# One PSUM tile per bank in the second layer, two-bank operations cut in two, buffers assigned by a table

## The chip, the cores and the metric

The kernel runs on one core of a Trainium2 chip. The metric is the device time of one execution in microseconds; the median of three runs is shown, and one more execution was taken with the hardware profiler. TensorE is called PE here (PEld is its weight load), VectorE is DVE, ScalarE is ACT, GpSimd is POOL and SyncE is SP.

## The reference

Three stages in a row, all in fp32, on 4 batches of 576 tokens (2304 tokens), model width 512, inner width 1536:

```python
x = _attn_ref(q, k, v, phi)              # attention over 32 memory slots
x = x.transpose(0, 2, 1, 3).reshape(2304, 512)
x = (x @ w_a) * (x @ w_b) @ w_out        # first layer
g = x @ w_gate                           # second layer
return (g * (1 / (1 + np.exp(-g)))) * (x @ w_val) @ w_out2
```

## The kernel before

**Stages.** Attention and the first layer fill the first 405 us. The second layer (from 405 us to the end) is written as units. A unit `U b.i` is one batch `b` (0 to 3) and one slice `i` (12 to 23) of 128 inner columns. It forms the gate and value columns for 576 tokens from seven products of half-size blocks instead of eight; each product (`product(n)`) is six matmuls of 128x288, since every fp32 operand is split in a high and a low part. Units of batches 0 and 1 run side by side for all `i`, then those of batches 2 and 3, so there are 24 pairs of units and 48 units. `H j.i.t` is a tile of the last matmul: 6 matmuls of 128x512, 108 such tiles in all, spread between the units; its result is added into an SBUF sum (line 829).

**PSUM in the second layer.** Each of the two units that run side by side (`o` is 0 or 1) has one PSUM tile of three banks, `chain0` or `chain1`; the banks are called A, C and Z. A third tile of two banks serves the `H` tiles, which use its banks in turn:

```python
for o in range(2):
    chain.append(ps2.tile([128, 3, 512], FP32, tag=f"chain{o}", name=f"chain{o}"))
chain.append(ps2.tile([128, 2, 512], FP32, tag="p4", name="p4"))
```

**The steps of a unit before,** in the order of the code, with the engine, the bank and the line. Product 5 into Z; ACT copies Z (769). Product 1 into A; ACT copies A to `gate` (774). Product 2 into C; DVE adds the copy onto C (778). Product 6 is accumulated onto A; ACT copies A (782). Product 3 is accumulated onto Z; DVE adds that copy onto Z (786). ACT takes the sigmoid of C and Z in one instruction of 576 elements (789), DVE multiplies by it, 576 elements (791). Product 7 is accumulated onto A; DVE writes A plus the copy of Z into C (795). Product 4 is accumulated onto A; DVE multiplies A and C by the result of 791, 576 elements (799). ACT casts the result to its high part (805), DVE forms the low part (807). Lines 761 and 507 are the matmuls of the products and of the `H` tiles.

**Order and waits.** The order of all instructions is written out as a list of words, `PLAN`, that a search made; each word runs one step of a generator, and each engine takes its instructions in the order of the list. Waits between engines are put in by the tile framework: it follows which instruction reads and writes which tile. Buffers come from pools that hand out the next free one. Weights of the second layer are decoded during the first pass (lines 209 to 262), stored to DRAM, and read again for each pass (lines 144 to 167). Words `z` are matmuls of the identity whose result nobody reads (`warm`, line 700); there are 15 in the list, most of them near its start.

Of the kernel before, what the change touches and what calls it, by code (L numbers as in the profile page):

```python
# [18 lines left out]
def kernel(  # L19
# [21 lines left out]
    nc = tc.nc  # L41
# [20 lines left out]

    ident = const.tile([128, 128], FP32, name="ident")
# [35 lines left out]
    def bank2(name):  # L99
        return ps.tile([128, 2, 512], FP32, tag="b2", name=name)  # L100
# [30 lines left out]
    def w_hi(i, grp, x):  # L131

        k = GRP[grp][1]
        shape = [128, k, 2, 256]
        if grp in ("g", "u"):
            t = w_p.tile(shape, FP32R, tag="w", name=f"w_{grp}")
        elif "w2" not in late:
            n = 0 if grp == "t" else 1024
            t = half("h10 1", FP32R).rearrange("p a b -> p (a b)")
            t = t[:, n:n + k * 512].rearrange("p (k l f) -> p k l f", l=2, f=256)  # L140
        else:
            t = late["w2"].tile(shape, FP32R, tag=grp, name=f"w_{grp}")
        wb[i, grp] = t
        nc.scalar.copy(out=t[:, :, 0], in_=x)  # L144
# [5 lines left out]
    def o_hi(i, x):  # L150
        t = w_p.tile([128, 2, DM], FP32R, tag="o", name="o")
# [7 lines left out]
    def again(i):  # L159

        s = raw_p.tile([128, 4, 256], FP32, tag="raw", name="again_s")
# [3 lines left out]
        else:  # L165
            a = raw_p.tile([128, 3, 256], FP32, tag="raw", name="again_a")
# [9 lines left out]
    def again_out(i):  # L176
        o = raw_p.tile([128, DM], FP32, tag="raw", name="again_o")
# [7 lines left out]
    def chunk_load(c):  # L185
# [3 lines left out]
        t = raw_p.tile([128, 512, 2], I32, tag="raw", name="raw")  # L189
# [125 lines left out]
    def att_phi(b):  # L315
# [3 lines left out]
        m = at_p.tile([128, PR, M], FP32, tag="pm", name="pm")  # L319
# [5 lines left out]
        nmx = sm_p.tile([128, 2, 1], FP32, tag="nmx", name="nmx")  # L325
# [39 lines left out]
        rs = sm_p.tile([128, 2], FP32, tag="rs", name="rs")  # L365
# [3 lines left out]
        kv = at_p.tile([128, 3, 2, D], FP32, tag="kvm", name="kvm")  # L369
# [48 lines left out]
    def att_scores(b, t):  # L418
# [31 lines left out]
        mx = sm_p.tile([128, 2, R, 1], FP32, tag="mx", name="mx")  # L450
# [8 lines left out]
        den = sm_p.tile([128, 2, R, 1], FP32, tag="den", name="den")  # L459
# [60 lines left out]
    def vw_part(parts):  # L520
# [19 lines left out]
        for part, pv in zip(parts, pvs):  # L540
            f, b = part[0]
            if f > 1 or b not in vw_2:
                vw_2[b] = [
                    vw_p.tile([128, 2, 2, 256], FP32R, tag=f"vw{x}", name=f"vw{x}") for x in "hl"
                ]
            t = vw_2[b]
            o = int(f == 1)
            for n, (f, b) in enumerate(part):
                vw_t[b, f] = [x[:, o + n] for x in t]
            n = len(part)  # L550
            hi, lo = [x[:, o:o + n].rearrange("c n g x -> c g n x") for x in t]
            nc.scalar.copy(out=hi, in_=pv[:, :, 0:n])
            yield
            nc.vector.tensor_tensor(out=lo, in0=pv[:, :, 0:n], in1=f32(hi), op=ALU.subtract)
# [21 lines left out]
    def s1_b(b, f):  # L576
        pb = s1_product(b, f, 128, "s1b")
        yield
        bs = bs_p.tile([128, 2, HB], FP32, tag="t", name="bs")
# [6 lines left out]
        if n not in g_t:  # L586
            g_t[n] = [g_p.tile([128, 2 * S], FP32R, tag=f"g{x}", name=f"g{x}") for x in "hl"]
        g = [of_batch(x, half) for x in g_t[n]]
        nc.scalar.copy(out=g[0], in_=bs)
        yield  # L590
        eng("gl", B * f + b).tensor_tensor(out=g[1], in0=bs, in1=f32(g[0]), op=ALU.subtract)
# [137 lines left out]
    def second():  # L729
# [7 lines left out]
        for o in range(2):  # L737
            chain.append(ps2.tile([128, 3, 512], FP32, tag=f"chain{o}", name=f"chain{o}"))
        chain.append(ps2.tile([128, 2, 512], FP32, tag="p4", name="p4"))
        yield  # L740

    def unit(b, i):
        o, j = b % 2, b // 2

        def bank(n, m=1):
            p = chain[o][:, n:n + m, 0:HB]
            return p if m > 1 else p[:, 0]
# [17 lines left out]

        product(5)
        yield
        q5 = late["tmp"].tile([128, HB], FP32, tag="q", name="p5")
# [4 lines left out]
        g = late["tmp"].tile([128, 2, HB], FP32, tag="g", name="gate")  # L773
# [22 lines left out]
        yield  # L796
        product(4)
        yield
        tt(out=g, in0=bank(A, 2), in1=s, op=mul)  # L799
        yield  # L800
        if (j, i) not in g2_t:
            g2_t[j, i] = late["g2"].tile([128, 2, 2 * S], FP32R, tag="g2", name="g2")
# [7 lines left out]
    def s4_tile(j, i, t):  # L810
        cs = slice(t * 128, (t + 1) * 128)
        p = chain[2][:, t % 2]
# [26 lines left out]
    def x_of(b):  # L839
# [3 lines left out]
        if not temps:  # L843
            temps.append(late["g2"].tile([128, 2, UNIT], FP32, tag="g2", name="temp"))
# [238 lines left out]
```

## Time and profile before

| | |
|---|---|
| median of 3 runs | 982.66 us (977.31 to 985.5) |
| profiled execution: its own time | 991.04 us |
| its span, first to last instruction | 989.3 us |
| granted TensorE clock, mean over the span | 0.969 of full speed |
| PE busy, PEld busy | 863.1 us (87%), 772.3 us (78%) |
| DVE, ACT, POOL busy | 570.7, 401.8, 378.1 us |

A profiled execution is a single one, so its parts are summed against its own 991.04 us. Matmuls are pipelined: the busy time of PE counts the tail of each matmul beside the next one's start.

### The profile page before, as it was taken

What the parts mean: (1) busy time and instruction counts of PE and PEld (TensorE: products, weight loads), DVE (VectorE), ACT (ScalarE), POOL (GpSimd) and SP (SyncE); (2) the same over time, 40 slices, a digit from 0 to 9 for tenths busy, and PEclk for the clock granted to TensorE, in tenths of its full rate; (3) what the DMA queues carried; (4) which work ended last, traced back from release to release, by engine and by line L of the source; (5) the groups of instructions that cost most, each with busy time, mean ns of one, the idle gap of its engine ahead of it and who ended that gap; (6) DMA issues with size and microseconds to landing.
All of it is one profiled execution on the core that took longest, in us unless ns stands there. A gap on an engine that the chain in (4) does not pass through costs nothing.

```text
span 989.3 us, 16445 instructions
## 1 busy us (share of the span) xinstructions
PE 863.1 (87%) x6570; PEld 772.3 (78%) x6570; DVE 570.7 (58%) x924; ACT 401.8 (41%) x742; POOL 378.1 (38%) x319
## 2 busy tenths in 40 slices
PE   5899999999999999877879797888878887897876
PEld 4688999999999999766668676777768776786764
DVE  5789858777866667653345555446543244444353
ACT  3666555444544445445343433335334423232220
POOL 0445554445434355544244343433431322232100
PEclk9799999999999999998799999999999999999999
DMA  9963333443322124125233433320242120111103
GB/s 331 345 209 102 130 99 122 138 145 99 131 92 86 64 78 127 64 91 169 82 105 92 127 128 101 103 91 1 70 129 70 59 85 1 49 59 38 38 1 95
DMA packets 61772, 102.51 MB, mean 104 GB/s; under 512 B 6400, under 2 KB 35072, under 8 KB 61696
## 3 DMA queue, kind: packets, MB, share of 16 engines
q1 hardware_dynamic: 60896, 100.29, 31.4%
q8 instruction: 51, 0.84, 0.3%
q10 hardware_dynamic: 800, 1.18, 0.3%
q14 instruction: 25, 0.20, 0.1%
HBM read 82.58 MB, written 18.87 MB: 103 GB/s over the span
## 4 chain that ended last, share of the span: by engine, by line
PE 75%; DVE 12%; ACT 5%; issue 3%; DMA 2%; SPq 1%; POOL 1%; DVEq 0%; ACTq 0%; POOLq 0%
PE chain L761 25%; PE p L507 15%; PE s L507 12%; PE s1a L515 7%; PE s1b L515 7%; DVE h_2x L829 3%; PE vw L530 2%; PE s L515 2%; DVE g L807 2%; DVE gate L799 1%; DVE sig L791 1%; DMA raw<-in_moe_w_b_dram 1%; ACT gate L774 1%; PE sc L429 1%; ACT gate L782 1%
## 5 line engine op out<-in xcount | busy, mean ns | idle before, releaser
L507 PE MATMUL p<-o,g 128*128 128x512 f32 x648 | 175.6, 412 | 11.9 <-DVE h_2x L829 10.4
L507 PEld LDWEIGHTS p<-o,g 128*128 128x128 f32 x648 | 122.9, 199 | 40.7 <-DVE h_2x L829 16.1
L507 PE MATMUL s<-gh,o 128*128 128x384 f32 x480 | 126.4, 335 | 0.0
L829 DVE TENSOR_TENSOR h_2x<-p,h_2x 128x512 f32<-128x512 f32 (+1 forms) x100 | 61.4, 633 | 65.1 <-PE p L507 65.0
L235 POOL TENSOR_TENSOR dec_a<-dec_a,raw 128x512 int32<-128x512 int32 x48 | 64.1, 1339 | 89.9 <-DVE dec_a L223 60.7
L507 PEld LDWEIGHTS s<-gh,o 128*128 128x128 f32 x480 | 87.1, 188 | 0.4 <-DVE dec_a L219 0.4
L209 ACT ACTIVATE dec_a<-raw 128x512 f32<-128x512 f32 x72 | 48.0, 674 | 83.8 <-POOL w L233 22.6
L507 PE MATMUL s<-gl,o 128*128 128x384 f32 x240 | 80.3, 334 | 0.0
L515 PE MATMUL s1b<-h_1x,vwh 128*128 128x288 f32 x384 | 67.6, 298 | 0.3 <-DVE h_1x L488 0.3
L515 PE MATMUL s1a<-h_1x,vwh 128*128 128x288 f32 x384 | 67.3, 297 | 0.0
L786 DVE TENSOR_TENSOR chain<-chain,gate 128x288 f32<-128x288 f32 x48 | 22.3, 465 | 74.9 <-PE chain L761 72.4
L761 PE MATMUL chain<-h_x0x,w_g 128*128 128x288 f32 x288 | 48.7, 310 | 17.1 <-ACT gate L774 13.7
L148 POOL TENSOR_TENSOR w_g<-again_a,w_g 128x512 fp32r<-128x512 f32 x24 | 31.0, 1293 | 81.9 <-ACT w_g L144 81.9
L761 PE MATMUL chain<-h_x0x,w_u 128*128 128x288 f32 x288 | 49.1, 315 | 14.9 <-DVE sig L791 9.3
L799 DVE TENSOR_TENSOR gate<-chain,sig 128x576 f32<-128x576 f32 x48 | 35.9, 755 | 43.7 <-PE chain L761 39.8
L761 PEld LDWEIGHTS chain<-h_x0x,w_g 128*128 128x128 f32 x288 | 42.4, 196 | 23.1 <-ACT gate L774 17.4
L148 POOL TENSOR_TENSOR w_u<-again_s,w_u 128x512 fp32r<-128x512 f32 x24 | 31.1, 1296 | 76.2 <-ACT w_u L144 76.2
L761 PE MATMUL chain<-h_x1x,w_t 128*128 128x288 f32 x288 | 48.7, 307 | 13.1 <-DVE chain L778 8.7
L761 PE MATMUL chain<-h_x1x,w_g 128*128 128x288 f32 x288 | 48.3, 306 | 13.5 <-ACT gate L774 11.1
L761 PE MATMUL chain<-h_x1x,w_u 128*128 128x288 f32 x288 | 46.8, 305 | 15.1 <-DVE sig L791 13.1
L515 PEld LDWEIGHTS s1b<-h_1x,vwh 128*128 128x128 f32 x384 | 56.8, 188 | 2.7 <-issue 0.8
L761 PEld LDWEIGHTS chain<-h_x0x,w_u 128*128 128x128 f32 x288 | 43.3, 201 | 19.8 <-DVE sig L791 11.7
(209 smaller groups left out, 1929.2 us busy)
## 6 DMA issues: line engine op xcount, KB each, us to landing
raw<-in_moe_w_out_dram SPq DMA_DIRECT2D x24, 512.0 KB, 3.9
again_s<-dr_w SPq DMA_DIRECT2D x24, 512.0 KB, 4.4
dr_w<-dec_a SPq DMA_DIRECT2D x36, 256.0 KB, 2.6
again_a<-dr_w SPq DMA_DIRECT2D x24, 384.0 KB, 3.1
raw<-in_moe_w_a_dram SPq DMA_DIRECT2D x12, 512.0 KB, 3.8
raw<-in_moe_w_b_dram SPq DMA_DIRECT2D x12, 512.0 KB, 4.7
raw<-in_moe_w_val_dram SPq DMA_DIRECT2D x12, 512.0 KB, 3.9
raw<-in_moe_w_gate_dram SPq DMA_DIRECT2D x12, 512.0 KB, 3.9
```

The costliest lines, as they stand in the source:

```text
L148: nc.gpsimd.tensor_tensor(out=t[:, :, 1], in0=x, in1=f32(t[:, :, 0]), op=ALU.subtract)
L209: nc.scalar.activation(out=f32(a), in_=f32(hi), func=ACTF.Abs)
L235: nc.gpsimd.tensor_tensor(out=a, in0=a, in1=lo, op=ALU.add)
L429: nc.tensor.matmul(pc[cols, o, r * M:(r + 2) * M], lhsT=qT_t[b][:, j * (R // 2) + r // 2, cols], rhs=kb[b % 2][:, g, j].rearrange("c o m - ...
L507: nc.tensor.matmul(dst, lhsT=l, rhs=r, start=(i == 0), stop=(i == n - 1))
L515: nc.tensor.matmul(p[:, hb, 0:HB], l, x, start=(i == 0), stop=(i == n - 1))
L530: nc.tensor.matmul(pv[M * j:M * j + M, g, n], lhsT=vt[b][rows, M * j:M * j + M], rhs=whl[f][0][rows, j].rearrange("p t c -> p (t c)"), sta ...
L761: nc.tensor.matmul(bank(where), lhsT=x, rhs=y, start=first and t == 0, stop=t == len(terms) - 1, skip_group_check=True,)
L786: tt(out=bank(Z), in0=bank(Z), in1=g[:, 1], op=add)
L799: tt(out=g, in0=bank(A, 2), in1=s, op=mul)
L807: tt(out=lo, in0=v, in1=f32(hi), op=ALU.subtract)
L829: tt(out=dst, in0=src, in1=dst, op=add)
```

## The change

- Each bank of the second layer's PSUM is a tile of its own: `p_a0`, `p_c0`, `p_z0` for one unit, `p_a1`, `p_c1`, `p_z1` for the other, `p_h0` and `p_h1` for the `H` tiles.
- An instruction then can't span banks A and C or C and Z. The sigmoid, the multiplication by it and the last multiplication become two instructions of 288 elements each. The half on C now follows right behind the addition onto C, ahead of product 6; the half on Z follows behind the addition onto Z.
- Buffers of most pools are taken by a table (`SLOTS`): the n-th tile of a kind gets the buffer that the table names. Their numbers stay as they were.
- In the first layer the low halves of two kinds of tiles (`vwl`, `gl`) are taken when they are first written, not together with the high halves.
- The list of the order is another one throughout. The words `z` are gone from it.

```diff
+    SLOTS = """
...
+    bs 012101201201021201211020201102110120021102101202 gh
...
+    def ring(pool, shape, dt, tag, name, key=None):
+
+        key = key or tag
+        n = made[key] = made.get(key, -1) + 1
+        if key in slots:
+            return pool.tile(shape, dt, tag=f"{tag}_{slots[key][n]}", bufs=1, name=name)
+        return pool.tile(shape, dt, tag=tag, name=name)
...
-        for o in range(2):
-            chain.append(ps2.tile([128, 3, 512], FP32, tag=f"chain{o}", name=f"chain{o}"))
-        chain.append(ps2.tile([128, 2, 512], FP32, tag="p4", name="p4"))
+        for n in ("a0", "c0", "z0", "a1", "c1", "z1", "h0", "h1"):
+            chain.append(ps2.tile([128, 512], FP32, tag=n, name=f"p_{n}"))
         yield
...
-        def bank(n, m=1):
-            p = chain[o][:, n:n + m, 0:HB]
-            return p if m > 1 else p[:, 0]
+        def bank(n):
+            return chain[3 * o + n][:, 0:HB]
...
         tt(out=bank(C), in0=bank(C), in1=g[:, 0], op=add)
         yield
+        s = ring(t_p, [128, 2, HB], FP32, "s", "sig")
+        nc.scalar.activation(out=s[:, 0], in_=bank(C), func=ACTF.Sigmoid)
+        yield
         product(6)
         yield
         nc.scalar.copy(out=g[:, 1], in_=bank(A))
         yield
+        tt(out=s[:, 0], in0=bank(C), in1=s[:, 0], op=mul)
+        yield
         product(3)
         yield
         tt(out=bank(Z), in0=bank(Z), in1=g[:, 1], op=add)
         yield
-        s = late["tmp"].tile([128, 2, HB], FP32, tag="s", name="sig")
-        nc.scalar.activation(out=s, in_=bank(C, 2), func=ACTF.Sigmoid)
-        yield
-        tt(out=s, in0=bank(C, 2), in1=s, op=mul)
+        nc.scalar.activation(out=s[:, 1], in_=bank(Z), func=ACTF.Sigmoid)
         yield
         product(7)
         yield
         tt(out=bank(C), in0=bank(A), in1=q5, op=add)
         yield
+        tt(out=s[:, 1], in0=bank(Z), in1=s[:, 1], op=mul)
+        yield
         product(4)
         yield
-        tt(out=g, in0=bank(A, 2), in1=s, op=mul)
+        tt(out=g[:, 1], in0=bank(C), in1=s[:, 1], op=mul)
+        yield
+        tt(out=g[:, 0], in0=bank(A), in1=s[:, 0], op=mul)
         yield
...
     def s4_tile(j, i, t):
         cs = slice(t * 128, (t + 1) * 128)
-        p = chain[2][:, t % 2]
+        p = chain[6 + t % 2]
...
     PLAN = """
-    z11 P0 p0 p0 p0 P1 W0.0 p1 p0 K0 z9 z7 p1 c0.0 L0 Q0 c0.0 W0.1 z8 p0 p1 p0 z10 c0.1 c0.0 e0
+    P0 K0 W0.1 p0 p0 c0.1 p0 p0 L0 c0.1 W0.0 p0 p0 e0 p0 Q0 P1 c0.1 p0 c0.1 c0.0 W1.1 p0 W1.2 q0.0
...
```

**PE in the second layer, the units of slice 13.** Rows are matmuls: the bank's tile, the token and weight tiles, the shape, how many in a row, and in brackets the engines whose semaphore the row waits for. Weights `w_g` belong to products 1 and 2, `w_t` to 6 and 3, `w_u` to 5 and 7. Before, from product 2 of the second unit to product 7 of the first:

```order
L761 MATMUL chain1_4867<-h2_x0x_4751,w_g_4948 128x288 [waits Activation_49]
L761 MATMUL chain1_4867<-h2_x0x_4751,w_g_4948 128x288 x5
L761 MATMUL chain0_4866<-h3_x0x_4643,w_t_5001 128x288 x6
L761 MATMUL chain1_4867<-h6_x0x_4800,w_t_5001 128x288 [waits DVE_49]
L761 MATMUL chain1_4867<-h6_x0x_4800,w_t_5001 128x288 x5
L761 MATMUL chain1_4867<-h4_x0x_4695,w_t_5001 128x288 [waits Activation_49]
L761 MATMUL chain1_4867<-h4_x0x_4695,w_t_5001 128x288 x5
L761 MATMUL chain0_4866<-h3_x0x_4643,w_u_4907 128x288 [waits DVE_49]
L761 MATMUL chain0_4866<-h3_x0x_4643,w_u_4907 128x288 x5
L761 MATMUL chain0_4866<-h1_x0x_4636,w_u_5084 128x288 x2
L761 MATMUL chain0_4866<-h1_x0x_4636,w_u_5084 128x288 [waits Pool_49]
```

Now, from product 2 of both units to product 6 and 3 of both:

```order
L789 MATMUL p_c0_4839<-h0_x0x_4565,w_g_4919 128x288 x6
L789 MATMUL p_c1_4842<-h2_x0x_4723,w_g_4919 128x288 x6
L789 MATMUL p_a0_4838<-h1_x0x_4583,w_t_4967 128x288 [waits Activation_49]
L789 MATMUL p_a0_4838<-h1_x0x_4583,w_t_4967 128x288
L789 MATMUL p_a0_4838<-h1_x0x_4583,w_t_4967 128x288 [waits Pool_49]
L789 MATMUL p_a0_4838<-h1_x0x_4583,w_t_4967 128x288 x3
L789 MATMUL p_a1_4841<-h6_x0x_4770,w_t_4967 128x288 [waits Activation_49]
L789 MATMUL p_a1_4841<-h6_x0x_4770,w_t_4967 128x288 x5
L789 MATMUL p_z1_4843<-h4_x0x_4644,w_t_4967 128x288 x6
L789 MATMUL p_z0_4840<-h3_x0x_4634,w_t_4967 128x288 x6
L789 MATMUL p_a0_4838<-h3_x0x_4634,w_u_4908 128x288 [waits Activation_49]
L789 MATMUL p_a0_4838<-h3_x0x_4634,w_u_4908 128x288 x5
```

Product 2 (`w_g`, into C) has lost its wait for ACT and stands for both units ahead of product 6; product 3 (`w_t`, into Z) has lost its wait for ACT; product 6 (`w_t`, onto A) waits for ACT, which copied A, and no longer for DVE.

**DVE at the same place.** Rows are the additions and multiplications of both units: 778, 786, 795, 791 and 799 before. Before:

```order
L786 TENSOR_TENSOR chain0_4866<-chain0_4866,gate_5049 128x288 [waits PE_49,Activation_49]
L778 TENSOR_TENSOR chain1_4867<-chain1_4867,gate_5076 128x288 [waits Activation_49]
L791 TENSOR_TENSOR sig_5100<-chain0_4866,sig_5100 128x576 [waits Activation_49]
L786 TENSOR_TENSOR chain1_4867<-chain1_4867,gate_5076 128x288 [waits PE_49,Activation_49]
L795 TENSOR_TENSOR chain0_4866<-chain0_4866,p5_5027 128x288 [waits DVE_49,PE_49]
L791 TENSOR_TENSOR sig_5134<-chain1_4867,sig_5134 128x576 [waits Activation_49]
L799 TENSOR_TENSOR gate_5049<-chain0_4866,sig_5100 128x576 [waits DVE_49,PE_49]
L795 TENSOR_TENSOR chain1_4867<-chain1_4867,p5_5031 128x288 [waits DVE_49,PE_49]
L219 TENSOR_SCALAR dec_a_5029<-dec_a_5029 128x512
L223 SCALAR_TENSOR_TENSOR dec_a_5029<-raw_4692,dec_a_5029 128x512 [waits DVE_49]
L799 TENSOR_TENSOR gate_5076<-chain1_4867,sig_5134 128x576 [waits PE_49]
```

Now lines 807, 820 and 826 are the additions, 816 and 828 the multiplications by the sigmoid, 832 and 834 the last multiplications:

```order
L807 TENSOR_TENSOR p_c0_4839<-p_c0_4839,gate_5043 128x288 [waits PE_49,Activation_49]
L807 TENSOR_TENSOR p_c1_4842<-p_c1_4842,gate_5048 128x288 [waits PE_49,Activation_49]
L816 TENSOR_TENSOR sig_5080<-p_c1_4842,sig_5080 128x288 [waits Activation_49]
L816 TENSOR_TENSOR sig_5069<-p_c0_4839,sig_5069 128x288
L820 TENSOR_TENSOR p_z1_4843<-p_z1_4843,gate_5048 128x288 [waits PE_49,Activation_49]
L820 TENSOR_TENSOR p_z0_4840<-p_z0_4840,gate_5043 128x288 [waits PE_49,Activation_49]
L826 TENSOR_TENSOR p_c0_4839<-p_a0_4838,p5_5015 128x288 [waits DVE_49,PE_49]
L828 TENSOR_TENSOR sig_5069<-p_z0_4840,sig_5069 128x288 [waits Activation_49]
L826 TENSOR_TENSOR p_c1_4842<-p_a1_4841,p5_5032 128x288 [waits PE_49]
L832 TENSOR_TENSOR gate_5043<-p_c0_4839,sig_5069 128x288 [waits DVE_49]
L834 TENSOR_TENSOR gate_5043<-p_a0_4838,sig_5069 128x288 [waits PE_49]
L828 TENSOR_TENSOR sig_5080<-p_z1_4843,sig_5080 128x288 [waits Activation_49]
```

The multiplication on C (816) now stands ahead of the addition onto Z, and the addition that writes C (826) stands ahead of the multiplication on Z (828), not behind it.

**PE at the start of the program.** `mx` is the maximum of `phi`, `kv` the products of attention's first batch. Before:

```order
L700 MATMUL warm_138<-ident_72 128x256 [waits Pool_49]
L323 MATMUL mx_148<-ident_72,pm_142 128x128 [waits DVE_49]
L332 MATMUL mx_148<-ident_72,nmx_150 64x128 [waits DVE_49]
L332 MATMUL mx_148<-ident_72,nmx_150 64x128
L700 MATMUL warm_167<-ident_72 128x256
L700 MATMUL warm_169<-ident_72 128x256
L323 MATMUL mx_171<-ident_72,pm_156 128x128 [waits DVE_49,PE_49]
L700 MATMUL warm_183<-ident_72 128x256 [waits PE_49]
L700 MATMUL warm_189<-ident_72 128x256 [waits PE_49]
```

Now:

```order
L349 MATMUL mx_151<-ident_72,pm_145 128x128 [waits DVE_49,Pool_49]
L358 MATMUL mx_151<-ident_72,nmx_155 64x128 [waits DVE_49]
L358 MATMUL mx_151<-ident_72,nmx_155 64x128
L377 MATMUL kv_173<-h0x_140,h9x_138 32x128 [waits DMAHW1_49,DMAHW2_49,DMAHW0_49,Activation_49]
L377 MATMUL kv_173<-h0x_140,h9x_138 32x128 x3
L377 MATMUL kv_173<-h1x_159,h9x_138 32x128 [waits DMAHW5_49,DMAHW4_49]
L377 MATMUL kv_173<-h1x_159,h9x_138 32x128 x3
```

The matmuls of `warm` are gone, and the second batch's `mx` stands later.

## Rows read from the trace of the kernel before

**Rows 1.** The chain that ended last: share of the span by engine.

```profile
PE 75%; DVE 12%; ACT 5%; issue 3%; DMA 2%; SPq 1%; POOL 1%; DVEq 0%; ACTq 0%; POOLq 0%
```

**Rows 2.** Stretches of the span: busy PE, PEld, DVE, ACT, POOL; clock, DMA.

```profile
0.00:100.00 100.00, 84.54 (x1343) 68.76 (x1343) 76.34 (x148) 53.17 (x93) 40.06 (x38) 0.93 0.73 246
100.00:405.00 305.00, 304.87 (x2565) 294.88 (x2565) 224.37 (x321) 141.64 (x226) 151.46 (x119) 1.00 0.34 109
405.00:437.00 32.00, 22.78 (x149) 19.98 (x148) 15.81 (x29) 15.47 (x31) 13.64 (x11) 1.00 0.20 66
437.00:500.00 63.00, 50.28 (x254) 42.83 (x252) 25.71 (x45) 26.59 (x54) 25.74 (x24) 0.84 0.37 113
500.00:967.00 467.00, 387.81 (x2218) 337.38 (x2219) 220.95 (x371) 164.26 (x337) 147.19 (x127) 0.97 0.22 71
967.00:990.00 23.00, 12.81 (x51) 8.52 (x50) 7.52 (x12) 0.67 (x1) 0.00 (x0) 1.00 0.38 103
```

**Rows 3.** Waits of PE in the second layer: releaser, us in total, times, longest.

```profile
PE chain L761 <- ACT gate L774: 24.9, 26, 2.3
...
PE chain L761 <- DVE sig L791: 22.4, 17, 2.9
...
PE chain L761 <- DVE chain L778: 14.3, 17, 2.4
...
PE chain L761 <- ACT gate L782: 10.5, 20, 1.5
PE p L507 <- DVE h_2x L829: 10.4, 15, 1.4
PE chain L761 <- ACT p L769: 10.3, 11, 2.7
...
PE chain L761 <- DVE gate L799: 5.3, 5, 1.4
PE chain L761 <- DVE chain L795: 5.3, 9, 1.2
```

**Rows 4.** Timeline at 611 and 621 us: start, duration, instruction, idle before and releaser.

```profile
611.54 0.76 DVE L791 TENSOR_TENSOR sig<-chain,sig 128x576 f32<-128x576 f32 x1 [0.72 <-ACT sig L789]
612.35 1.07 PE L761 MATMUL chain<-h_x0x,w_u 128*128 128x288 f32 x6 [0.35 <-DVE sig L791]
...
621.64 0.40 ACT L774 COPY gate<-chain 128x288 f32<-128x288 f32 x1 [3.24 <-DVE g L807]
622.09 1.87 PE L761 MATMUL chain<-h_x0x,w_g 128*128 128x288 f32 x12 [1.94 <-ACT gate L774]
```

**Rows 5.** Groups by shape: busy us, mean ns of one, idle before them.

```profile
L223 DVE SCALAR_TENSOR_TENSOR dec_a<-raw,dec_a 128x512 int32<-128x512 int32 x72 | 54.6, 758 | 2.5
...
L829 DVE TENSOR_TENSOR h_2x<-p,h_2x 128x512 f32<-128x512 f32 x80 | 54.2, 687 | 60.3 <-PE p L507 60.2
...
L807 DVE TENSOR_TENSOR g<-gate,g 128x576 fp32r<-128x576 f32 x48 | 43.5, 907 | 8.4 <-ACT g L805 8.0
...
L791 DVE TENSOR_TENSOR sig<-chain,sig 128x576 f32<-128x576 f32 x48 | 36.0, 753 | 15.8 <-ACT sig L789 15.4
...
L789 ACT ACTIVATE sig<-chain 128x576 f32<-128x576 f32 x48 | 31.2, 653 | 57.1 <-DVE chain L786 57.1
...
L786 DVE TENSOR_TENSOR chain<-chain,gate 128x288 f32<-128x288 f32 x48 | 22.3, 465 | 74.9 <-PE chain L761 72.4 <-issue 2.6
...
L774 ACT COPY gate<-chain 128x288 f32<-128x288 f32 x48 | 19.2, 400 | 56.1 <-DVE g L807 40.6 <-PE chain L761 15.0
```

**Rows 6.** Pieces of the chain in the second layer: start, us, what.

```profile
604.38 1.06 PE chain L761 x6
605.45 1.37 PE p L507 x6
...
644.85 1.59 PE chain L761 x12
```

**Rows 7.** The group of the `warm` matmuls.

```profile
L700 PE MATMUL warm<-ident 128*128 128x256 f32 x30 | 12.5, 527 | 5.3 <-ACT h0x L502 3.8 <-POOL ident masks.py:199 1.4
```

More of the change, by code (lines that the diff above doesn't have):

```diff
@@ L99, in bank2 @@
     def bank2(name):
-        return ps.tile([128, 2, 512], FP32, tag="b2", name=name)
+        return ring(ps, [128, 2, 512], FP32, "b2", name)
     def f32(ap):
@@ L135, in w_hi @@
         if grp in ("g", "u"):
-            t = w_p.tile(shape, FP32R, tag="w", name=f"w_{grp}")
+            t = ring(w_p, shape, FP32R, "w", f"w_{grp}")
         elif "w2" not in late:
@@ L141, in w_hi @@
         else:
-            t = late["w2"].tile(shape, FP32R, tag=grp, name=f"w_{grp}")
+            t = ring(late["w2"], shape, FP32R, grp, f"w_{grp}")
         wb[i, grp] = t
@@ L150, in o_hi @@
     def o_hi(i, x):
-        t = w_p.tile([128, 2, DM], FP32R, tag="o", name="o")
+        t = ring(w_p, [128, 2, DM], FP32R, "o", "o")
         ohl[i] = t[:, 0], t[:, 1]
@@ L188, in chunk_load @@
         w = mats[i // NF][j].bitcast(I32)
-        t = raw_p.tile([128, 512, 2], I32, tag="raw", name="raw")
+        t = ring(raw_p, [128, 512, 2], I32, "raw", "raw")
         if j < 2:
@@ L318, in att_phi @@
         x = phi_t[b]
-        m = at_p.tile([128, PR, M], FP32, tag="pm", name="pm")
+        m = ring(at_p, [128, PR, M], FP32, "pm", "pm")
         over_r(eng("rmx", b), m, x, ALU.max)
@@ L324, in att_phi @@
         yield
-        nmx = sm_p.tile([128, 2, 1], FP32, tag="nmx", name="nmx")
+        nmx = ring(sm_p, [128, 2, 1], FP32, "nmx", "nmx")
         nc.vector.tensor_reduce(
@@ L368, in att_phi @@
         yield
-        kv = at_p.tile([128, 3, 2, D], FP32, tag="kvm", name="kvm")
+        kv = ring(at_p, [128, 3, 2, D], FP32, "kvm", "kvm")
         for g in range(2):
@@ L578, in s1_b @@
         yield
-        bs = bs_p.tile([128, 2, HB], FP32, tag="t", name="bs")
+        bs = ring(bs_p, [128, 2, HB], FP32, "t", "bs", "bs")
         nc.scalar.copy(out=bs, in_=pb)
@@ L586, in s1_b @@
         if n not in g_t:
-            g_t[n] = [g_p.tile([128, 2 * S], FP32R, tag=f"g{x}", name=f"g{x}") for x in "hl"]
-        g = [of_batch(x, half) for x in g_t[n]]
+            g_t[n] = [ring(g_p, [128, 2 * S], FP32R, "gh", "gh")]
+        g = [of_batch(g_t[n][0], half)]
         nc.scalar.copy(out=g[0], in_=bs)
         yield
+        if len(g_t[n]) < 2:
+            g_t[n].append(ring(g_p, [128, 2 * S], FP32R, "gl", "gl"))
+        g.append(of_batch(g_t[n][1], half))
         eng("gl", B * f + b).tensor_tensor(out=g[1], in0=bs, in1=f32(g[0]), op=ALU.subtract)
@@ L764, in product @@
                 )
+        t_p = late["tmp"]
         product(5)
         yield
-        q5 = late["tmp"].tile([128, HB], FP32, tag="q", name="p5")
+        q5 = ring(t_p, [128, HB], FP32, "q", "p5")
         nc.scalar.copy(out=q5, in_=bank(Z))
@@ L772, in unit @@
         yield
-        g = late["tmp"].tile([128, 2, HB], FP32, tag="g", name="gate")
+        g = ring(t_p, [128, 2, HB], FP32, "g", "gate")
         nc.scalar.copy(out=g[:, 0], in_=bank(A))
```

383 lines of the change are left out of this document (204 added, 179 removed).

## The prediction

> **What bounds the kernel now.** I read first the chain of work that ended last: 75% of the span is PE, 12% DVE, 5% ACT [rows 1]. So PE sets the time, but not everywhere. The stretches say where it doesn't [rows 2]. From 100 to 405 us PE is busy for 304.9 of 305 us: first layer, PE-bound, nothing but less PE work helps there. From 405 us to the end it is busy for 22.8 + 50.3 + 387.8 + 12.8 = 473.7 of 585 us, and no other engine comes near (DVE 270 us). A stretch in which no engine is full is bound by waits, so I read next what PE waited for there [rows 3].
>
> Five of those rows are waits that the data don't ask for. Line 774 copies bank A; the PE group that waits for it 26 times (24.9 us) is `w_g`, product 2, which writes bank C. The timeline shows one: the copy of A runs from 621.64 to 622.04, and the `w_g` group starts at 622.09, PE having sat idle for 1.94 us [rows 4]. Likewise product 7 writes A, whose last reader was the copy 782, yet it starts at 612.35, right behind the multiplication 791 on C and Z that ends at 612.30 [rows 4]. In the same way product 6 (A) waits for the addition 778 on C, product 3 (Z) for the copy 782 of A, and products on A for the copy 769 of Z. All these share one thing: the waiting product writes another bank of the same three-bank tile. So waits here go by tile, not by bank, and a unit runs as one string: product, DVE or ACT, product, DVE or ACT. The `H` tiles have it too: two banks, one tile, so an `H` tile waits for the addition 829 of the tile just before it, not of the one before that (10.4 us).
>
> **What PE needs at least.** When products follow each other without a gap, two of them take 1.59 us, 0.795 each; an `H` tile takes 1.37 us [rows 6]. The second layer has 48 x 7 = 336 products and 108 `H` tiles: 336 x 0.795 + 108 x 1.37 = 267 + 148 = 415 us, in a stretch of 584 us.
>
> The Trainium skill (Perfetto Trace Analysis, section Identifying the Most-Contended Engine) says that busy time of matmuls is a bad measure of headroom and the busy share of weight loads a good one. By the busy time 585 - 473.7 = 111 us could go. By the weight loads, which fill 294.9 of 305 us (96.7%) where PE never idles and 19.98 + 42.83 + 337.38 + 8.52 = 408.7 us here, the layer would need 423 us [rows 2], and 162 us could go. The trace agrees with the rule: 423 is near the 415 that the products give, and 473.7 isn't.
>
> **The change, part by part.**
>
> *One tile per bank.* It removes the five waits and the one of the `H` tiles: 24.9 + 22.4 + 14.3 + 10.5 + 10.3 + 10.4 = 92.8 us in 106 waits [rows 3]. Each of these also breaks the pipeline: a product that starts from rest takes 1.06 us in the chain, not 0.795 [rows 6], so 106 x 0.265 = 28.1 us more. Bounds: nothing, if what comes next is as late, and the whole 121 us.
>
> What is late next? For product 2 its bank's last reader of the unit before, long done; for product 3 the copy 769, three steps back; for product 7 the copy 782. These leave room: a unit's longest string of true needs is product 1, copy, product 6, copy, product 7, addition, product 4, multiplication: four products 3.2, two copies 0.8, two DVE steps 0.93, with hops of 0.05 some 5.3 us, against 14 x 0.795 + 4.5 x 1.37 = 17.3 us of PE work in a pair of units. Waits for real needs stood at 5.3 + 5.3 us before [rows 3]; with PE earlier they grow. I let a third of the removed 92.8 us come back, 31 us.
>
> *Two-bank operations in two.* DVE: 288 elements take 465 ns, 576 take 753 [rows 5], so each cut adds 2 x 465 - 753 = 177 ns; two cuts per unit, 48 units: 17.0 us. ACT: 576 elements of the sigmoid take 653, and no row has 288; the copy of 288 takes 400, so 0 to 147 ns a unit, 0 to 7 us; I take the upper end, the copy being of the same engine, source and size. Both lie beside PE work: DVE goes from 270 to 287 us of 585, ACT has 207. They cost nothing on the path as long as PE isn't waiting for that DVE step; if it is, they cost their 17 us. The cut also shortens the path: C is finished and its sigmoid taken while products 6 and 3 run, and the addition 795 no longer stands behind the sigmoid and multiplication of Z, so product 4 follows product 7 by one addition (0.47 us) where before the string put 0.65 + 0.75 + 0.47 us between products 3 and 4 beside product 7. That is part of the waits counted above.
>
> *Clock.* PE's granted clock is 0.84 of full from 437 to 500 us and 0.97 up to 967 [rows 2]; with levels of 1.2 and 2.4 GHz these are 0.32 x 63 + 0.06 x 467 = 48 us at the lower one, all in the layer in which PE idles, while it is 1.00 where PE is full. Up to half of 48 us is lost there; much of it is idle anyway, so I take 8 us back.
>
> *Order and buffers of the first layer.* From 100 to 405 us PE is full before, so an order can only lose there; the table keeps the numbers of buffers. In the first 100 us PE idles for 15.5 us and the clock is 0.93 [rows 2]. The `warm` matmuls that go were 12.5 us of PE [rows 7], mostly in idle time. A gain of 10 (fewer of them, earlier loads) and a loss of 8 (a longer stretch at the lower clock) both fit; I take -3.
>
> **The sums,** against the profiled execution's 991.0 us (span 989.3 and 1.7 around it). From the waits: 991.0 - 92.8 - 28.1 - 8 + 31 - 3 = 890. From the work: first layer 405 - 3 = 402; PE work 415; the idle time at 405 to 437 us, where no `H` tiles exist yet to fill in, 9.2; half of the 12.7 us idle at 437 to 500, where weights are decoded; 5 us for the end, where the last unit's steps and the last store stand alone; 1.7: 839. The first counts only waits that were seen and lets a third come back; the second supposes that nothing in the steady part waits. Nothing in the rows sets one above the other, so I take the middle, 865. The profiled execution ran 991.0 where the median is 982.7; times 0.9915, **857 us**.
>
> **Rivals.**
>
> *DVE's queue takes the place of the tile.* Each unit hands over from DVE to PE at four places (banks A, C and Z come free, and 795 before product 4), and DVE also carries the `H` additions of 687 ns, low parts of 907 and decoding steps of 758 [rows 5] in one fixed order. If at half of the 192 handovers PE waits for one other step of 465 ns and starts its pipeline again (0.265), that is 96 x 0.73 = 70 us on the 839: 909, or 901 us after the correction. For it: PSUM has no spare bank in this layer, and DVE goes to 287 of some 450 us. Against it: in the first layer DVE is as busy (224 of 305 us, 74%) and PE never waits [rows 2].
> The Trainium skill (PSUM — Partial Sum Buffer, section Engine vs sequencer instructions) says that the queues of ScalarE and VectorE are strictly first in, first out, which is this rival's mechanism: a freed instruction gains nothing behind one that still waits. The trace agrees as far as it goes: no row shows a DVE step overtaking another. It gives the rival the chance below, and no other time.
>
> *The units stay strings.* If the split tiles were still waited for as one, or the new order kept each unit's steps in line, the waits would stay and the cuts would lie on the string: per unit 2 x 177 + 147 ns and three more hops of 0.05 [rows 4, 5], 0.65 us; each of the two strings holds 24 units, 16 us: 1007, or **998 us**, slower. It decides if the first five rows of waits [rows 3] are all still there. Against it: in the new order product 2 and product 3 carry no wait for ACT at all.
>
> *A cold start.* Without `warm` the lower clock lasts twice as long as before (0.07 x 2 x 100 = 14 us at it): 10 us more than I took, 867 us. It is inside the range.
>
> **How the numbers follow.** The forecast 0.66 (828 to 885), DVE's queue 0.25 (885 to 920), the cold start 0.07, strings 0.02. Low end: the sum from the work, 839 x 0.9915 = 832, less 4 for a better start. High end: the queue's 901 and 7 for the first layer. Range 828 to 908, which leaves out what of the queue's case lies above it, the strings, and a little below. About 1% is what a measurement of this kernel tells from no change. Faster by over 1%: forecast, queue and cold start, less some room for what I didn't see: 0.95; within 1%: 0.02; slower: 0.03.
>
> **What the changed kernel's profile would show.** Right, if waits of `w_g` on the copies of A and of `w_u` on the multiplication by the sigmoid are gone, if the second layer takes 420 to 480 us with weight loads above 85% busy, if its clock is near 1.00, and if the first layer still ends at 395 to 410 us. The queue's rival would show as PE waits on 826, 828 and 834, and DVE above 65% in the second layer. The prediction is wrong if PE sits idle there for over 100 us again, whatever it waits for, or if the first layer moves by over 10 us.

## The result and the profile after

The changed kernel takes 833.89 us (median of 4 runs, 832.53 to 836.04) where the kernel before took 980.86 beside it; the ratio is 0.8501, interval 0.8458 to 0.8545. The profiled execution took 836.0 us with a span of 834.2. The prediction was 857 us, range 828 to 908.

The chain that ended last, in the changed kernel: PE's share was 75% [rows 1].

```profile
PE 92%; DVE 3%; DMA 1%; ACT 1%; SPq 1%; issue 1%; DVEq 0%
```

The stretches of the changed kernel, with the columns of [rows 2]: span, busy PE, PEld, DVE, ACT, POOL; granted clock, DMA share, GB/s.

```profile
0.00:100.00 100.00, 77.77 (x1307) 66.14 (x1307) 71.36 (x142) 49.22 (x86) 34.51 (x34) 0.88 0.69 235
100.00:405.00 305.00, 304.66 (x2565) 294.43 (x2555) 230.44 (x330) 145.50 (x233) 157.57 (x122) 1.00 0.34 109
405.00:437.00 32.00, 28.71 (x208) 28.18 (x208) 21.56 (x44) 19.46 (x42) 18.99 (x17) 1.00 0.43 136
437.00:500.00 63.00, 63.00 (x402) 58.63 (x402) 43.46 (x88) 40.34 (x91) 41.70 (x38) 1.00 0.58 191
500.00:810.00 310.00, 309.78 (x1975) 288.65 (x1974) 192.71 (x395) 147.22 (x335) 130.36 (x110) 1.00 0.28 87
810.00:835.00 25.00, 20.04 (x101) 16.89 (x99) 13.50 (x26) 2.58 (x5) 0.00 (x0) 0.96 0.36 95
```

From 437 to 810 us PE is busy for 372.8 of 373 us, at full clock. Before, this layer was the one in which no engine was full; now it looks like the first layer. From the first product of the second layer to the last matmul the trace before gives 407.1 to 985.0 us, the one after 410.9 to 830.0: 577.9 us have become 419.1. Idle stretches of PE over 0.05 us add up to 105.0 us in 124 places there before, to 0.6 us in 2 places now.

What PE waits for in the changed kernel (releaser, us in total, times, longest), against [rows 3]:

```profile
PE p_a L789 <- ACT gate L814: 0.4, 1, 0.4
...
PE p_h L533 <- DVE h_2x L864: 0.2, 1, 0.2
```

Lines 814 and 864 are the second copy of bank A and the addition of an `H` tile. Nothing else of the second layer stands in the list but 2.9 us ahead of its first product. The longest wait of the whole list, 9.1 us in two places, lies in the first attention, before 23 us. The timeline of the changed kernel shows why (start, duration, instruction, idle before):

```profile
631.81 0.40 ACT L803 COPY gate<-p_a 128x288 f32<-128x288 f32 x1 [1.32 <-DVE g L842]
...
631.96 0.96 PE L789 MATMUL p_c<-h_x1x,w_g 128*128 128x288 f32 x6
```

The copy of A runs until 632.21, and product 2 starts on C at 631.96, in the middle of it. Before, product 2 started 0.05 us after the end of that copy [rows 4].

The cut operations in the changed kernel (busy us, mean ns of one, idle before), against [rows 5], one half of the sigmoid on ACT and then steps of DVE:

```profile
L810 ACT ACTIVATE sig<-p_c 128x288 f32<-128x288 f32 x48 | 19.4, 413 | 15.1 <-DVE p_c L807 14.6
```

```profile
L842 DVE TENSOR_TENSOR g<-gate,g 128x576 fp32r<-128x576 f32 x48 | 38.1, 799 | 17.6 <-ACT g L840 17.0
...
L816 DVE TENSOR_TENSOR sig<-p_c,sig 128x288 f32<-128x288 f32 x48 | 21.0, 450 | 9.3 <-ACT sig L810 9.0
```

### The profile page after: what moved, and what is told of

It reads as the page before. It is cut to its first block, busy times and chain, and to the rows that moved or that the text cites. A ratio compares the mean times of both kernels' runs of the same rounds, so it can differ in the third digit from the quotient of the medians.

```text
span 834.2 us, 16467 instructions
## 1 busy us (share of the span) xinstructions
PE 804.0 (96%) x6540; PEld 752.9 (90%) x6540; DVE 573.0 (69%) x1020; ACT 404.3 (48%) x790; POOL 383.1 (46%) x319
## 4 chain that ended last, share of the span: by engine, by line
PE 92%; DVE 3%; DMA 1%; ACT 1%; SPq 1%; issue 1%; DVEq 0%
PE p_a L789 18%; PE p_h L533 18%; PE s L533 15%; PE s1b L541 9%; PE p_z L789 9%; PE s1a L541 9%; PE p_c L789 4%; PE s L541 3%; PE vw L556 3%; DMA raw<-in_moe_w_b_dram 1%; PE sc L455 1%; PE kv L377 1%; PE qT L437 1%; PE sc L465 0%; SPq L325 0%
## 5 line engine op out<-in xcount | busy, mean ns | idle before, releaser
L533 PE MATMUL p_h<-o,g 128*128 128x512 f32 x648 | 163.3, 393 | 0.2 <-DVE h_2x L864 0.2
L533 PEld LDWEIGHTS p_h<-o,g 128*128 128x128 f32 x648 | 117.0, 188 | 21.3 <-DVE h_2x L864 0.5
L864 DVE TENSOR_TENSOR h_2x<-p_h,h_2x 128x512 f32<-128x512 f32 (+1 forms) x100 | 62.0, 632 | 35.8 <-PE p_h L533 35.5
L259 POOL TENSOR_TENSOR w<-dec_a,raw 128x512 int32<-128x512 int32 x24 | 31.9, 1331 | 63.8 <-DVE dec_a L249 44.3
L541 PEld LDWEIGHTS s1a<-h_1x,vwh 128*128 128x128 f32 x384 | 56.5, 189 | 2.2 <-issue 1.2
L249 DVE SCALAR_TENSOR_TENSOR dec_a<-raw,dec_a 128x512 int32<-128x512 int32 x72 | 56.0, 778 | 2.5
L840 ACT CAST g<-gate 128x576 fp32r<-128x576 f32 x48 | 32.1, 676 | 38.9 <-PE p_h L533 22.8
L609 DVE TENSOR_TENSOR bs<-s1a,bs 128x576 f32<-128x576 f32 x48 | 35.9, 753 | 21.9 <-PE s1a L541 19.7
L842 DVE TENSOR_TENSOR g<-gate,g 128x576 fp32r<-128x576 f32 x48 | 38.1, 799 | 17.6 <-ACT g L840 17.0
L237 ACT ACTIVATE raw<-raw 128x512 int32<-128x512 uint32 x72 | 48.4, 679 | 0.0
```

What stands on the lines that cost most here:

```text
L237: nc.scalar.activation(out=lo, in_=lo.bitcast(U32), func=ACTF.Copy, scale=2.0 ** -29)
L249: nc.vector.scalar_tensor_tensor(out=a, in0=hi, scalar=-0x40000000, in1=a, op0=ALU.bitwise_and, op1=ALU.bitwise_or)
L533: nc.tensor.matmul(dst, lhsT=l, rhs=r, start=(i == 0), stop=(i == n - 1))
L541: nc.tensor.matmul(p[:, hb, 0:HB], l, x, start=(i == 0), stop=(i == n - 1))
L609: nc.vector.tensor_tensor(out=bs, in0=pa_t.pop((b, f)), in1=bs, op=ALU.mult)
L840: nc.scalar.copy(out=hi, in_=v)
```

## The experiments

**Theory:** the gain comes from waits by tile; with one tile per bank they go, whatever the order. **Rivals:** the new order makes the gain; the start of the kernel has part in it; DVE's queue is close behind. Each ratio is to runs of the kernel before on the same chip. The second layer's length is from its first product to the last matmul, its idle time the sum of PE's pauses over 0.05 us there; both are from the profiled execution.

| kernel | median us | ratio to before, interval | second layer us | PE idle there us, places |
|---|---|---|---|---|
| before | 980.9 to 985.9 | 1 | 577.9 | 105.0, 124 |
| changed | 833.9 | 0.850 (0.846 to 0.855) | 419.1 | 0.6, 2 |
| old_order_bank_tiles | 832.6 | 0.845 (0.841 to 0.849) | 421.9 | 2.0, 6 |
| old_order_cut_only | 990.1 | 1.005 (1.002 to 1.008) | 577.9 | 108.1, 126 |
| old_order_h_tiles | 960.4 | 0.976 (0.970 to 0.981) | 547.0 | 90.1, 105 |
| old_order_cz_tile | 849.2 | 0.862 (0.857 to 0.867) | 439.5 | 12.3, 26 |
| new_order_ac_tile | 903.6 | 0.918 (0.913 to 0.922) | 492.0 | 49.1, 55 |
| new_order_h_tile | 859.1 | 0.872 (0.869 to 0.875) | 444.0 | 15.3, 21 |
| new_order_no_table | 833.8 | 0.849 (0.846 to 0.852) | 420.1 | 0.4, 1 |
| old_start_new_second | 834.1 | 0.848 (0.845 to 0.851) | 422.3 | 2.1, 2 |
| old_order_no_warm | 829.8 | 0.844 (0.841 to 0.846) | 421.4 | 1.8, 5 |
| old_order_gap_filled | 832.2 | 0.846 (0.844 to 0.849) | 420.9 | 1.5, 4 |
| old_order_dve_load | 887.7 | 0.901 (0.896 to 0.906) | 475.9 | 37.2, 42 |
| old_order_dve_free | 878.7 | 0.893 (0.888 to 0.897) | 470.9 | 32.5, 28 |

**old_order_bank_tiles: the tiles without the order.** The kernel before with

```diff
-        for o in range(2):
-            chain.append(ps2.tile([128, 3, 512], FP32, tag=f"chain{o}", name=f"chain{o}"))
-        chain.append(ps2.tile([128, 2, 512], FP32, tag="p4", name="p4"))
+        for n in ("a0", "c0", "z0", "a1", "c1", "z1", "h0", "h1"):
+            chain.append(ps2.tile([128, 512], FP32, tag=n, name=f"p_{n}"))
...
-        nc.scalar.activation(out=s, in_=bank(C, 2), func=ACTF.Sigmoid)
+        for h, n in enumerate((C, Z)):
+            nc.scalar.activation(out=s[:, h], in_=bank(n), func=ACTF.Sigmoid)
...
-        tt(out=g, in0=bank(A, 2), in1=s, op=mul)
+        for h, n in ((1, C), (0, A)):
+            tt(out=g[:, h], in0=bank(n), in1=s[:, h], op=mul)
```

and the first multiplication cut in the same way.

> The kernel before, its order of work unchanged, with each PSUM bank of the second layer its own tile and the sigmoid and both multiplications cut in two where they stood. Theory (waits by tile): the 92.8 us of false waits and 28 us of pipeline restarts of the prediction go, and some of them comes back because DVE and ACT still take Z's steps before those of C: 860 to 925 us. Rival (the new order makes the gain): the tiles alone do little, 960 to 1000 us.

It takes 832.6 us, below the range of either expectation: the whole gain, with the order of before. Its second layer:

```profile
407.00:829.00 422.00, 419.79 (x2664) 389.53 (x2664) 274.90 (x548) 208.86 (x471) 192.62 (x162) 1.00 0.33 105
```

The rival that the new order makes the gain has fallen. The theory's figure was too careful too: nothing came back.

**old_order_cut_only: the cuts without the tiles.** The lines with `for h, n in` above, on the three-bank tiles.

> The kernel before, tiles and order unchanged, with only the sigmoid and both multiplications cut in two. Theory (units are strings, the cuts lie on them): 24 units in each of two strings by 0.65 us, 16 us longer, 993 to 1003 us, less where the pair's other unit fills the gap. Rival (the cuts are hidden): within 3 us of the kernel before. In either case no gain from the cuts alone.

0.5% slower (0.2 to 0.8%), 2 to 8 us, with the same 577.9 us of second layer in the profiled execution. That lies between the two expectations. The cuts alone gain nothing and cost at most about half of the 16 us of the strings rival.

**old_order_h_tiles: the `H` banks alone.**

```diff
-        chain.append(ps2.tile([128, 2, 512], FP32, tag="p4", name="p4"))
+        for n in ("h0", "h1"):
+            chain.append(ps2.tile([128, 512], FP32, tag=n, name=f"p_{n}"))
...
-        p = chain[2][:, t % 2]
+        p = chain[2 + t % 2]
```

> The kernel before with one edit: the two H banks are two tiles; the three-bank tiles, the order and the uncut operations stay. Theory (the prediction's term for the H tiles): 10.4 us of waits in 15 places and 15 restarts of 0.265 us go: 14 us less than the kernel before, a ratio of 0.983 to 0.990. Rival (the units stay strings, so PE waits at the next product instead): 0.996 to 1.004.

2.4% faster, 24 us, more than expected. The wait on the addition is gone, the other waits are what they were (25.0, 22.0, 14.3, 10.5 and 10.5 us on the five releasers that had 24.9, 22.4, 14.3, 10.5 and 10.3 [rows 3]), and PE idles 14.9 us less. It also pauses in 19 places less, some 5 us of restarts (0.27 us each, worked out under the sizes below). The term had 10.4 + 4.0. The rest is clock. In the stretch that had 0.84 [rows 2] it shows the first row here, and old_order_cut_only shows the second:

```profile
437.00:500.00 63.00, 46.36 (x275) 40.59 (x273) 29.94 (x50) 29.96 (x62) 29.30 (x27) 0.97 0.44 135
```

```profile
437.00:500.00 63.00, 48.81 (x266) 41.45 (x265) 27.26 (x57) 29.86 (x67) 25.57 (x24) 0.92 0.43 130
```

Not all of the rise from 0.84 is the edit's: old_order_cut_only has the tiles of before and idles for 108.1 us, and still shows 0.92. The matmuls that fill this stretch before (the 151st to the 400th of the second layer) take 62.9 us there, 59.6 in old_order_cut_only and 55.9 here. In the executions on that chip the mean clock of the span has a median of 0.981, against 0.975 for the kernel before; by the 9 us for each hundredth that the kernel before shows (below, under the clock) this is worth some 5 us. The three parts make some 25 us.

**new_order_ac_tile and new_order_h_tile: the false waits put back.** The changed kernel, with A and C of a unit in one tile,

```diff
+        for o in range(2):
+            t = ps2.tile([128, 2, 512], FP32, tag=f"ac{o}", name=f"p_ac{o}")
+            z = ps2.tile([128, 512], FP32, tag=f"z{o}", name=f"p_z{o}")
+            chain.extend((t[:, 0], t[:, 1], z))
```

or with the two `H` banks in one:

```diff
+        chain.append(ps2.tile([128, 2, 512], FP32, tag="p4", name="p4"))
...
-        p = chain[6 + t % 2]
+        p = chain[6][:, t % 2]
```

> The changed kernel, order and cut operations kept, with banks A and C of a unit in one two-bank tile again. Theory (waits by tile): product 2 waits for the copy of A again and product 6 for the addition and the sigmoid on C. In the changed kernel's trace the copy ends after the start of product 2 in 33 units (40.6 us in sum) and the sigmoid after the start of product 6 in 36 (37.1 us); with 0.265 us for each restart that is some 96 us: 890 to 940 us. Rival (the new order makes the gain): at most 845 us.

> The changed kernel with the two H banks in one tile again. Theory (waits by tile): 24 of the 108 H tiles directly follow another H tile and would wait for its addition (about 0.75 us with the hop) and restart PE (0.265): some 24 us, 850 to 865 us. Rival (the H tile's part is nothing, since products lie between): 834 to 838 us.

903.6 us and 859.1 us, both in the range of the theory. PE's waits in the first:

```profile
PE p_ac L793 <- ACT gate L807: 31.2, 28, 2.7
PE p_ac L793 <- ACT sig L814: 15.4, 18, 2.4
```

and in the second:

```profile
PE p L533 <- DVE h_2x L865: 14.0, 18, 1.5
```

They are the waits that the edit restores, on a copy of A, on a sigmoid of C and on the addition of the `H` tile before, with the order, the cuts and the table left as they were.

**old_order_cz_tile: two tiles a unit, the sigmoid uncut.** The kernel before with A in its own tile, C and Z in one of two banks, the sigmoid and the first multiplication whole, the last one cut, `H` in two tiles.

> The kernel before, its order unchanged: bank A its own tile, C and Z one tile with the sigmoid and the first multiplication uncut over both, the last multiplication cut, H banks two tiles. Theory (waits by tile): none of the false waits of the prediction joins two banks of C and Z, so all go: 830 to 845 us, and the cut of the sigmoid and of the first multiplication isn't needed. Rival (the addition before product 4 stands behind the sigmoid and the multiplication of both banks, 0.65 + 0.75 us, and PE waits for it): 850 to 900 us.

849.2 us, between the two forecasts: 17 us slower than with three tiles. PE's waits there:

```profile
PE p_cz L765 <- DVE p_cz L799: 3.1, 7, 0.8
PE p_a L765 <- DVE p_cz L799: 2.8, 5, 0.6
```

Line 799 is the addition that product 4 needs; it stands behind the sigmoid and multiplication of both banks, as the rival said (second row). DVE has that order in old_order_bank_tiles too, where PE waits for this addition once, for 0.6 us; so it is likely the uncut length of the two steps that costs here. The first row is a false wait that the theory had overlooked: the next unit's product 5, into Z, waits for an addition on C. Product 3 has another, 1.7 us in 4 places on the addition of line 778. So the third tile and the two cuts are worth some 17 us together.

**new_order_no_table, old_start_new_second: table and start.** The changed kernel with an empty table (buffers rotate); and that with the first layer in the order of before.

```diff
-    SLOTS = """
-    raw
-    0123021230120130231203210230120130230213203212130120231303210323103120120132103210321030321302310213203132321033013021031
...
+    SLOTS = """""".split()
```

> The changed kernel with its order, tiles and cuts, and buffers that rotate in each pool instead of going by the table. Theory (the table only says which buffer, and PE has work while one comes free): 832 to 837 us. Rival (the table keeps writers off buffers that are still read): 842 us or more, with waits of ACT or DVE on DMA or PE in its place.

> The changed kernel with the first layer in the order of before (warm matmuls too) and the second in the new order; buffers rotate, without the table. Theory (the start differs by 4 us, PE's products in the second layer begin at 406.9 against 410.9 us, and the new order needs 419.1 us there against 421.9): 828 to 831 us. Rival (the difference at the start is given back where the second layer waits for decoded weights): 833 to 836 us.

833.8 and 834.1 us: the first as its theory said, the second as its rival. The table is worth nothing that can be measured. The 4 us at the start don't belong to the order or the table: the same order began the second layer at 406.5 us without the table and at 406.9 with it (new_order_h_tile), instead of 410.9, in the profiled executions, and the medians are the same.

**old_order_no_warm, old_order_gap_filled: the start.** old_order_bank_tiles with the `warm` words taken out of the order; and with eleven matmuls instead of one in the `warm` step ahead of the idle time from 19.6 to 24.1 us:

```diff
-        nc.tensor.matmul(
+        for _ in range(11 if n == 6 else 1):
+            nc.tensor.matmul(
```

> The kernel of old_order_bank_tiles (old order, one tile per bank, cut operations) without the warm matmuls. Theory of the prediction (cold start): without them the lower clock lasts twice as long in the first 100 us, 7 us more at 832.6: 838 to 845 us. Rival (they do nothing, since the first layer's start is set by loads and by the chain of the first attention): 829 to 836 us.

> The kernel of old_order_bank_tiles with ten more warm matmuls where PE idles from 19.6 to 24.1 us; its granted clock is 0.91, 0.50, 0.50 and 0.73 in the four 5 us slices from 20 to 40 us. Theory (the fall follows that idle time and PE's speed counts there): the clock stays near 1.00, up to 6.8 us less: 825 to 829 us. Rival (the start is bound by loads, the DMA engines being busy all the time up to 50 us): 831 to 835 us.

829.8 and 832.2 us, both in the range of the rival. The same stretch in old_order_bank_tiles, in old_order_gap_filled, and in old_order_no_warm:

```profile
20.00:40.00 20.00, 15.06 (x262) 11.56 (x263) 11.49 (x25) 9.90 (x17) 6.60 (x7) 0.66 1.02 365
```

```profile
20.00:40.00 20.00, 16.04 (x292) 12.42 (x291) 14.80 (x34) 11.43 (x20) 6.61 (x7) 0.96 1.06 377
```

```profile
20.00:40.00 20.00, 15.04 (x286) 11.64 (x285) 16.13 (x36) 13.85 (x26) 7.42 (x8) 0.83 1.07 378
```

Filling the idle time kept the clock at 0.96 where it had been 0.66, and the time didn't move. The DMA engines are full (1.02 to 1.07) in all three; that the loads set the pace there is argued from this and was not tested by itself. Without the warm matmuls nothing is lost either, and the clock in this stretch is higher than with them (0.83 against 0.66). That kernel, the fastest of all, is 0.5% ahead of new_order_no_table on the same chip (829.8 against 833.8; 0.8409 to 0.8461 and 0.8457 to 0.8517), less than the 1% that I called measurable. But all five of its runs (827.6 to 830.5 us) lie below all five of old_order_gap_filled on that chip (831.0 to 833.2), so leaving the warm matmuls out may gain some 2 us.

**old_order_dve_load, old_order_dve_free: DVE's queue.** old_order_bank_tiles with the low part of each unit issued three times,

```diff
-        tt(out=lo, in0=v, in1=f32(hi), op=ALU.subtract)
+        for _ in range(3):
+            tt(out=lo, in0=v, in1=f32(hi), op=ALU.subtract)
```

and with it once, but four additions behind it on a tile of their own:

```diff
+        for _ in range(4):
+            tt(out=late["x"], in0=late["x"], in1=late["x"], op=add)
```

> The kernel of old_order_bank_tiles with the last DVE step of each unit, the low part, issued three times instead of once: 96 more of 907 ns, 87 us of DVE; DVE is busy for some 277 of the second layer's 422 us and would be for 364. Theory (DVE is far off the path, its order leaves room): at most 8 us more, 831 to 841 us. Rival (DVE's queue decides, as in the prediction's first rival): a step that PE waits for stands up to 1.8 us later, at half of 48 units and their H tiles 20 to 45 us and more: 853 to 900 us.

887.7 us, 55 us more: my theory, that DVE is far off the path, fell. The way in which it costs wasn't clear, for the repeated step also holds a gate buffer. ACT's wait for it in this kernel, 35.5 us in 28 places without the load:

```profile
ACT gate L772 <- DVE g L809: 113.8, 42, 4.7
```

So I formed another theory, that the buffers carry the cost, and loaded DVE without holding one.

> The kernel of old_order_bank_tiles with four more DVE additions of 256 elements behind each unit's low part, on a scratch tile that nothing else reads; about as much DVE time as in old_order_dve_load (192 steps of an estimated 0.4 to 0.45 us, from 465 ns for 288 elements: 77 to 86 us), but no gate buffer is held longer. In old_order_dve_load ACT waited 113.8 us for the low part before it could copy bank A into one of the two gate buffers (35.5 without the load) and PE 28.7 us for that copy. Theory (the cost there came through the gate buffers): 832 to 845 us here. Rival (it came through DVE's queue as such): 865 to 890 us, with PE waits on the additions and multiplications of DVE.

878.7 us: this theory fell as well. PE's waits in the kernel, and the group of the added steps:

```profile
PE p_a L761 <- DVE p_c L797: 9.0, 6, 3.3
PE p_h L507 <- DVE h_2x L834: 6.7, 5, 3.4
PE p_z L761 <- DVE sig L793: 5.2, 3, 2.5
```

```profile
L812 DVE TENSOR_TENSOR scr<-scr 128x256 f32<-128x256 f32 x192 | 116.7, 608 | 4.9
```

PE waits for additions and multiplications that stand behind the added ones. The load was larger than I had estimated, 116.7 us and not 77 to 86: half of the added steps took 0.43 us or less, as estimated, but some took up to 1.65 (last section). DVE is busy for 274.9 of 422 us of the second layer in old_order_bank_tiles (65%), where PE idles for 2 us; for 376.7 of 469 us here (80%), where it idles for 32.5. Where between these it begins to cost wasn't tried. That a held gate buffer costs something besides is likely (55 us for 133.7 - 44.1 = 89.6 us of added low parts there, 46 for 116.7 here), but the two kernels differ in more than that, and it stays open.

## Why the prediction was right

**The mechanism** was right in its main part. The false waits [rows 3] are gone with the tiles and their cuts in the old order (old_order_bank_tiles), come back with the tiles alone (new_order_ac_tile, new_order_h_tile), and don't go with the cuts alone (old_order_cut_only). The new order and the table are worth nothing that can be told.

**The sizes.** The second layer lost 577.9 - 419.1 = 158.8 us. Idle time accounts for 105.0 - 0.6 = 104.4. The rest, 54.4 us, is PE's busy time, 472.9 before and 418.4 now for the same matmuls: restarts and clock. How it divides can be estimated from the fourteen profiled executions. A linear fit to their second layers, of PE's busy time by the number of its pauses and by its busy time at the lower clock, gives 0.27 us for each pause and 0.46 us for each microsecond busy at the lower clock. It meets each kernel within 1.1 us but new_order_h_tile, which takes 2.9 us more: pauses ahead of `H` tiles may cost more. For the kernel before that is 34 us for 124 pauses and 20 us for the 44.3 us that PE was busy at the lower clock. The pair that differs least in clock agrees: old_order_cz_tile has 20 pauses more than old_order_bank_tiles and is busy for 426.7 against 419.8 us, at most 0.34 us a pause. So the 0.265 us that the prediction gave a restart is borne out; its 28.1 us counted 106 of the 124 pauses.

- *A third of the waits comes back, 31 us:* the step that failed. All waits behind the first product are 0.6 us together, and even those of before (5.3 + 5.3 us [rows 3]) are gone. The 17.3 us of PE work in a pair of units against a string of 5.3 us of true needs, which the prediction worked out, was the better guide.
- *Clock, 8 us:* about 20, by the fit above. The prediction's 48 us at the lower clock were right (47.8 in the trace), but "much of it is idle anyway" was wrong: PE is busy for 44.3 of them. Part of these 20 us belongs to the one profiled execution. The 36 runs of the kernel before beside the experiments go from 977.2 us at a mean clock of 0.981 to 990.8 at 0.968, by a straight line some 9 us for each hundredth, and the profiled one had 0.969 and 991.0 us.
- *The sum from the work, 839:* 836.0 measured, and some of that is luck. Its 415 us for the second layer, with 9.2 and 6.4 us of idle time at the start and 5 at the end, are 419.1 us and 4.2 behind it in the changed kernel: 11.5 us too many there meet a first product that came 8.9 us later than the 402 of the sum. The middle with 890 was the wrong choice: the sum from the work alone, times 0.9915, says 832 against 833.89. The factor too fitted the kernel before and its slow profiled execution; the changed kernel's is 833.89 / 836.04 = 0.997.
- The Trainium skill (Perfetto Trace Analysis, section Identifying the Most-Contended Engine) sets the busy share of weight loads above that of matmuls. By its rule I had 423 us for the layer; the trace agrees, with 419.1, and the weight loads are busy for 389.6 us of it, 93%. Two misses cancel in the 423: it supposed 408.7 us of weight loads, as before, and a share of 96.7%.
- *Cuts:* 17.0 us on DVE and 7 on ACT, beside PE. The sigmoid's cut costs (2 x 0.411 - 0.653) x 48 = 8.1 us of ACT, with 413 and 410 ns for its halves, those of DVE 2 x (2 x 449 - 754) x 48 = 13.8 us. DVE's sum rose by 2.3 us only (570.7 to 573.0), since other steps became shorter in the changed kernel, the low part from 907 [rows 5] to 799 ns in the mean among them (last section). PE idles for 0.6 us in the layer, so all of it was hidden, as forecast.
- *First layer, -3:* +3.8 (410.9 for 407.1 us) in the profiled execution, but 406.5 in that of new_order_no_table and 406.9 in that of new_order_h_tile, which have the same order there, the latter with the table: the difference is one between executions, and no median shows it.

**The rivals.** *DVE's queue* is real and wasn't reached: no wait of the second layer on 826, 828 or 834 in the changed kernel, DVE at 265.8 of 419 us (63%), but in the old order 15 points more of DVE, from 65 to 80%, cost 46 us. *Strings:* not what happened, and their 16 us were too many (2 to 8). *A cold start:* its premise didn't come. The clock of the first 100 us was 0.88 instead of 0.93 in the profiled execution of the changed kernel, but 0.93 in new_order_no_table, which has no warm matmuls either, and 0.97 in old_order_no_warm; and warm matmuls don't decide the time there (old_order_no_warm, old_order_gap_filled).

**The signs** named ahead came in the main: both waits gone, weight loads above 85%, clock 1.00. Two lay a little outside what was named: the second layer with 419 us under 420 to 480, and the first layer's end, 410.9, over 395 to 410.

## What to carry to other kernels

Where an engine waits for an instruction whose data it doesn't touch, look at what the two share: here a tile of several PSUM banks made 93 us of waits out of nothing, and naming the banks apart, with the operations cut that spanned them, gave the whole 15% without a new order. When such waits go and the work that is left beside them is long, predict from the work of the bounding engine, not from the waits that might return; test how much room the next engine has by loading it. Count with the gaps what they cost beside their idle time: here 105.0 us of idle time stood beside 54.4 us of longer busy time, restarts and clock.

## What was not expected of the hardware

- The clock came back as PE's pauses went (levels of 1.2 and 2.4 GHz). Its mean in the second layer is 0.96 to 0.98 in the kernels that idle there for 32 us and more, and 0.996 to 1.00 in those with 16 us or less. The time at the lower clock is hardly idle: PE is busy for 44.3 of 47.8 us of it in the kernel before.
- A higher clock can be worth nothing: 0.96 instead of 0.66 from 20 to 40 us, while the DMA engines were full, left the time as it was.
- Two kinds of DVE steps that have all operands in SBUF were slow at times, and only beside POOL. The 192 added additions of old_order_dve_free took 608 ns in the mean, but 426 in the median and up to 1649. The 137 that ran beside no POOL instruction took 410 to 428 ns, and all 38 that took over 490 overlapped one. The low part shows the same in the kernel before: 746 to 760 ns in the 31 units with no POOL instruction beside it, up to 1790 in the other 17, so its mean of 907 [rows 5] is a mixture. Two kinds with an operand in PSUM show nothing of it: the 256-element addition of the `H` tiles took 408 to 425 ns and the multiplication by the sigmoid (791) 746 to 760, beside POOL or not. This is read from where the steps overlap, with POOL's spans rough in a trace; no run changes POOL's work to test it.
